# A fused Mamba-2 and PReLU kernel: wider filler matmuls, two clamps moved to VectorE, a transposition issued later, products of pair 1 in another bank

## The chip, the cores and the metric

The kernel runs on one core of one Trainium2 chip. A core has five engines that work side by side, each taking its own instructions in order: TensorE (PE in the profile; its weight loads are shown apart as PEld), VectorE (DVE), ScalarE (ACT), GpSimd (POOL) and SyncE (SP), which here only issues DMA transfers. Engines wait for each other through semaphores. The metric is the device time of one execution in microseconds (us). Less is better.

## The reference

Two blocks follow each other.

1. A state-space block. For 4 batches and 8 heads, 768 tokens are taken in chunks. Inputs are x (32 wide), B and C (16 wide) and a decay a per token, clipped to 1e-6..1. In a chunk, `y_intra = ((C B^T) * L) x`, where L[i, j] is the product of the decays from j+1 to i for j <= i and 0 above. To it comes `y_inter = (C state) * decay_to_i`. The state then becomes `decay_full * state + sum_j B_j x_j decay_from_j`.
2. The result, as 3072 tokens of 256 features, goes through `h = x w_in` (256 x 2048), `g = max(h, 0) + alpha * min(h, 0)` and `g w_out` (2048 x 256). The weights come in as 64-bit floats and are brought to 32 bits on the chip.

## The kernel before

The order of every engine is written out by hand: the order of the calls in the source is the order of each engine's instructions. Nothing is reordered by cost. Tiles come from pools with a fixed number of buffers, and an allocation waits for the readers of the buffer's earlier tile.

**Tiles and stages.** The 24 chunks of 128 tokens are taken in 12 pairs. Four chunks (512 tokens) make a group for the second block. The first two pairs are done by `first_two()` with half chunks of 64 tokens, beside the start of the second block. Then a loop over `f` = 4..15 (line 1431) does the hidden blocks of group 0 (`hidden`, `output`) with later pairs' stages (`ssm`) between them. Groups 1 to 5 follow in the loop at line 1482, with a scheme that needs seven products in place of eight (`quad`, `product`, `combine`). The change touches only what comes before and around the start of the first loop.

**A weight piece** is 128 x 2 x 256 numbers. There are 16: `w_in` 0, 1, then alternately `w_in` and `w_out`. Its raw words are loaded by SyncE (`load_weights`, L253). `convert_a` takes the magnitude on ScalarE (L269), clamps it on GpSimd (L271), and prepares the low half on ScalarE (L276 for `w_in`, L279 for `w_out`; the latter reads `g_mul` and `g_add`, which `slope_signs` writes on GpSimd, L391). `sign` takes the sign on VectorE (L290), `convert_b` shifts and joins on VectorE (L300), and `convert` adds the halves on GpSimd (L322). `convert_next` calls `convert` for the next piece in order and may issue another load.

**Fillers.** `keep_warm` (L330) issues matmuls of ones that nothing reads, at four places before and in `first_two`: eight, six and four of 128 columns and two of 128 columns.

**Pair 1 in `first_two`.** `spread` (L859) brings decays to four banks `sp`, `scan` (L865) runs over them on VectorE, `turned` transposes B and C (L835) and copies them (L841 to L849). `added` (L887) makes the products B^T x for the states, in banks `dps`. `states` (L902) chains them on VectorE, `gram_of` (L874) makes C B^T, `times` (L879) multiplies it by the scanned decays, `mask` (L908) spreads the states, and `x_products` (L921) and `state_products` (L933) give y, which `copy_out` (L941, L942) puts into `xT`.

**Hidden blocks.** `hidden_two(g, f, t0, hp, after)` does blocks f and f + 1 for 256 tokens (L1088), calling `after` behind each of its four products; `scaled` (ScalarE, L1098) and L1109 (VectorE) apply the PReLU and free the bank `hp`. There are two such banks, taken in turn: `hidden_two(0, 0, 2 * Q)`, `hidden_two(0, 2, 2 * Q)` (lines 1418 and 1420), then `hidden(0, 4)` (L1073, with L1076 and L1077), `hidden(0, 5)` and so on.

**Rows.** `rows_scan(0)` (L457) scans the decays of 96 rows backwards on VectorE; `rows_turn` (L497) transposes the result on TensorE and copies it on ScalarE (L504) to `prt`, which `pair_loads` (L528, GpSimd) multiplies with B to `bn`. `rows_products` (L434) scans forwards and stores the result `rpf` to DRAM (L437, `pf`), from where `load_products` (L167) reads it spread over the partitions as `ap`. The stage of pair 2 that makes its states (L637) multiplies by `ap`.

**Pair 2's products** (`products_bc`, L737) use four banks, the last of them one of the two `hp` banks, in turn after `hidden(0, 7)`.

Of the kernel before, what the change touches and what calls it, by code (L numbers as in the profile page):

```python
# [9 lines left out]
F32 = mybir.dt.float32  # L10
U32 = mybir.dt.uint32
U16 = mybir.dt.uint16
ALU = mybir.AluOpType
ACTF = mybir.ActivationFunctionType

F64_INF, F64_ZERO = (struct.unpack("f", struct.pack("I", w))[0] / 8
                     for w in (0x47F00000, 0x38000000))
# [5 lines left out]
def kernel(  # L23
# [25 lines left out]
    nc = tc.nc  # L49
# [4 lines left out]
    batch, H, S, D = x.shape  # L54
    N = B.shape[-1]
    P = 128
    Q = 128
# [9 lines left out]
    GT = GC * Q  # L67
    NG = NCH // GC
    NP = NCH // 2
    LATE = 4  # L70
    WARM = 8
    NQ = NF // 2
    NZ = NF // 4
    HM = d_model // 2
# [180 lines left out]

    parts = {}

    def convert_a(dst, src, sg):

        if src.dtype == F32:  # L260
            return
        raw = raws.pop(id(dst))
        hi = raw[:, :, :, 1]
        half = raw.rearrange("p k w t -> p k (w t)").bitcast(U16)
        half = half.rearrange("p k (w t) -> p k w t", t=4)[:, :, :, 1]
        t = wtp.tile([P, 2, WQ], U32, name="wt")
        g = wtp.tile([P, 2, WQ], F32, name="wg")

        nc.scalar.activation(out=t.bitcast(F32), in_=hi.bitcast(F32), func=ACTF.Abs, scale=0.125)  # L269

        nc.gpsimd.tensor_scalar(out=t.bitcast(F32), in0=t.bitcast(F32), scalar1=F64_INF,  # L271
                            scalar2=F64_ZERO, op0=ALU.min, op1=ALU.max)


        if sg is None:
            nc.scalar.activation(out=g, in_=half, func=ACTF.Copy, scale=2.0**-11, bias=2.0**25)  # L276
        for i in range(2 if sg is not None else 0):
            f = slice(sg + i, sg + i + 1)
            nc.scalar.activation(out=g[:, i], in_=half[:, i], func=ACTF.Identity,  # L279
                                 scale=g_mul[:, f], bias=g_add[:, f])  # L280
        parts[id(dst)] = hi, t, g

    signs = {}

    def sign(dst, src, sg):

        if src.dtype == F32 or id(dst) in signs:
            return
        r = wtp.tile([P, 2, WQ], U32, name="wr")
        nc.vector.tensor_single_scalar(out=r, in_=parts[id(dst)][0], scalar=SIGN,  # L290
                                       op=ALU.bitwise_and)
        signs[id(dst)] = r

    def convert_b(dst, src, sg):

        if src.dtype == F32:
            return
        sign(dst, src, sg)
        (hi, t, g), r = parts.pop(id(dst)), signs.pop(id(dst))
        nc.vector.scalar_tensor_tensor(out=r, in0=t, scalar=3, in1=r,  # L300
                                       op0=ALU.logical_shift_left, op1=ALU.bitwise_xor)
        parts[id(dst)] = r, g
# [24 lines left out]
    def keep_warm(to, n, cols=2 * Q):  # L327

        for i in range(n):
            nc.tensor.matmul(to[:, :cols], warm.to_broadcast([P, P]), warm.to_broadcast([P, cols]),  # L330
                             start=True, stop=True, skip_group_check=True)

    keep_warm(ps_h.tile([P, GT], F32, name="hp"), WARM, Q)
    ident = const.tile([P, P], F32, name="ident")
    make_identity(nc, ident)

# [115 lines left out]
    def rows_scan(i):  # L452

        d0 = held[i]
        nc.vector.memset(d0[:, Q : Q + 1], 0.0)
        pr = prep.tile([RW, Q], F32, name="pr")
        nc.vector.tensor_tensor_scan(out=pr[:, ::-1], data0=d0[:, 1 : Q + 1][:, ::-1],  # L457
                                     data1=ends[:RW, ::-1], initial=0.0,
                                     op0=ALU.mult, op1=ALU.add)
        return pr  # L460
# [55 lines left out]
    def pair_loads(gp):  # L516

        b, c = divmod(2 * gp, CPB)
        nat, abc, xt, ap = loads["p", gp]

        bn = work.tile([P, 2, H * N], F32, name="bn")
        i, bi = divmod(b, 2)
        if gp >= HALF:
            pj = prt[i].rearrange("p (j b m h) -> p j b m h", j=2, b=2, h=H)[:, :, bi, c // 2]
        else:
            pj = (prt[i if gp >= NB else "short"]
                  .rearrange("p (b h c) -> p b c h", b=2, h=H)[:, bi, c : c + 2])
        nc.gpsimd.tensor_tensor(  # L528
            out=bn.rearrange("p k (h n) -> p k h n", h=H),
            in0=nat[:, 0].rearrange("p k (h n) -> p k h n", h=H),  # L530
            in1=pj.unsqueeze(3).to_broadcast([P, 2, H, N]), op=ALU.mult)
        return bn
# [8 lines left out]
    def spare():  # L541

        return ps_h.tile([P, GT], F32, name="hp", tag="hp")
# [272 lines left out]
    def first_two():  # L816
# [47 lines left out]
        def scan(i, r, t):  # L864
            nc.vector.tensor_tensor_scan(out=dec[i][:, r], data0=t[:, : 2 * Q], data1=ident_q,  # L865
                                         initial=0.0, op0=ALU.mult, op1=ALU.add)
# [15 lines left out]
        def added(dps, bn, xt):  # L882
            for k in range(2):
                for r in range(4):
                    rs = slice(32 * r, 32 * r + 32)
                    for j, hs in enumerate(halves):
                        nc.tensor.matmul(dps[j][rs, k], bn[hs, k, rs],  # L887
                                         xt[hs, k, 2 * r * D : 2 * (r + 1) * D],
                                         start=True, stop=True, tile_position=(HQ * j, 32 * r),
                                         skip_group_check=True)  # L890
# [4 lines left out]
        def states(i, dps, pf, cs=range(4)):  # L895
            for c in cs:
                if i == 0 and c == 0:
                    nc.scalar.copy(out=new[0][:, 0], in_=dps[0][:, 0])
                    continue
                e = (c + 1) * HQ - 1  # L900
                old = new[i][:, c - 1] if c else new[0][:, 3]
                nc.vector.scalar_tensor_tensor(out=new[i][:, c], in0=old, scalar=pf[:, e : e + 1],  # L902
                                               in1=dps[c % 2][:, c // 2], op0=ALU.mult,
                                               op1=ALU.add)
# [85 lines left out]


        hp = spare()
        keep_warm(hp, 6, Q)
        gram_of(bc0, cz0, sp)
        dps = dps_in([hp, tp])
        added(dps, bn0, xt0)
# [4 lines left out]
        for r in (2, 3):  # L1001
            times(0, r, sp[r])
        z1 = first_a(loads["a", 1], nc.vector, lent[1][:, 2:])
        convert_a(*pieces[0])
        sign(*pieces[0])
        convert_b(*pieces[0])
        y = places([ss(), ss()], [hp, tp])
        x_products(y, xt0, 0, (0,))
        sp = [bank(r) for r in range(4)]
        keep_warm(sp[0], 4, Q)  # L1010
        x_products(y, xt0, 0, (1,))
        state_products(y, 0, cd0)
        spread(z1, sp)
        keep_warm(sp[3][:, 2 * Q :], 2, Q)
        convert_next()
        convert_a(*pieces[1])
        xts[0] = xtp.tile([P, KC, GT], F32, name="xT")
        copy_out(0, y)
        sign(*pieces[1])
        convert_b(*pieces[1])  # L1020
        prelu_of = {0: hidden_two(0, 0, 0, spare())}


        for r in range(4):
            scan(1, r, sp[r])
        bn1 = pair_loads(1)
        convert_next(first=False)
        mask(0, slice(3, 4))
        own = [ss(), ss()]
        bc1, cz1 = turned(nat1, own[0], nc.scalar)  # L1030
        dps = [t.rearrange("p (k m) -> p k m", k=2)
               for t in (own[1][:, 2 * Q : 2 * Q + 4 * D], sp[3][:, : 4 * D])]
        added(dps, bn1, xt1)
        cd1 = decayed_c(bc1, pf1)

        def among(i, k):
            if (i, k) == (0, 1):
                states(1, dps, pf1)
                gram_of(bc1, cz1, sp)
                one_at_a_time(1, range(3))  # L1040
                for r in range(4):
                    times(1, r, sp[r])
                prelu_of[0]()
                convert_a(*pieces[2])
                sign(*pieces[2])
            if (i, k) == (1, 0):
                y = places(own, [bank(0), bank(1)])
                x_products(y, xt1, 1)
                state_products(y, 1, cd1)
                copy_out(1, y)  # L1050

        prelu_of[2] = hidden_two(0, 2, 0, spare(), among)
        convert_next(first=False)
        mask(1, slice(3, 4))
        slope_signs()
        prelu_of[2]()
        pr = rows_scan(0)
        rows_products()
        load_products(NB, loads["p", NB][3])
        rows_turn(0, pr)  # L1060
        state[0] = new[1][:, 3]
        masked[0] = sm[1][:, 3]
        early[0] = 16
# [337 lines left out]
    def convert_next(first=True, **kw):  # L1401


        i = done[0]
        if i < len(pieces):
            convert(*pieces[i], **kw)
            if first and i and i + 2 < len(pieces):
                convert_a(*pieces[i + 2])
            if loaded[0] == i + 6:
                load_next()  # L1410
        done[0] += 1
# [6 lines left out]
    hidden_two(0, 0, 2 * Q, spare())()  # L1418
    convert_next(first=False)
    rest = hidden_two(0, 2, 2 * Q, spare())  # L1420
    convert_a(*pieces[4])
    rest()
    identity_bank()
# [133 lines left out]
```

## Time and profile before

| what | us |
|---|---|
| median of 3 executions | 364.32 |
| lowest and highest of them | 363.22, 364.84 |
| the profiled execution's own time | 365.23 |
| its span, first to last instruction | 362.4 |
| TensorE busy | 353.2 (97%) |
| VectorE busy | 238.7 (66%) |
| GpSimd busy | 203.5 (56%) |
| ScalarE busy | 171.3 (47%) |

The profile lists for each instruction its engine, its source line (L12 is line 12), the operation, what it writes and reads, its start and its length. "Idle before" is time in which the engine had nothing to run, with the engine that ended it. The chain of work that ended last is followed back from the last instruction, at each step to what released it by the recorded semaphore events; such a releaser is inferred and can be a bystander that ended at the same time. The granted clock is the share of TensorE's full clock. "SPq" is SyncE issuing a transfer; "issue" is time for which the profile shows no cause.

### The profile page before, as it was taken

What the parts mean: (1) busy time and instruction counts of PE and PEld (TensorE: products, weight loads), DVE (VectorE), ACT (ScalarE), POOL (GpSimd) and SP (SyncE); (2) the same over time, 40 slices, a digit from 0 to 9 for tenths busy, and PEclk for the clock granted to TensorE, in tenths of its full rate; (3) what the DMA queues carried; (4) which work ended last, traced back from release to release, by engine and by line L of the source; (5) the groups of instructions that cost most, each with busy time, mean ns of one, the idle gap of its engine ahead of it and who ended that gap; (6) DMA issues with size and microseconds to landing.
All of it is one profiled execution on the core that took longest, in us unless ns stands there. A gap on an engine that the chain in (4) does not pass through costs nothing.

```text
span 362.4 us, 7825 instructions
## 1 busy us (share of the span) xinstructions
PE 353.2 (97%) x3011; PEld 290.5 (80%) x3011; DVE 238.7 (66%) x487; ACT 171.3 (47%) x386; POOL 203.5 (56%) x226
## 2 busy tenths in 40 slices
PE   8869999999999999999999999999999999999996
PEld 7647656667888888888888888888888888888885
DVE  7874795989846756766656866657866634743363
ACT  2345756634345435535535535535535534453431
POOL 5853658669965947544546545537545546334510
PEclk9996999999999999999999999999999999999999
DMA  7889689704535510510540530530201001001102
GB/s 118 178 172 328 221 162 344 164 5 76 171 64 135 98 39 25 107 46 11 109 88 12 108 87 14 112 81 17 58 2 31 0 2 29 2 0 32 31 0 58
DMA packets 105581, 30.24 MB, mean 83 GB/s; under 512 B 79896, under 2 KB 101448, under 8 KB 105544
## 3 DMA queue, kind: packets, MB, share of 16 engines
q1 hardware_dynamic: 105160, 29.57, 35.5%
q8 instruction: 23, 0.38, 0.4%
q10 hardware_dynamic: 384, 0.18, 0.2%
q14 instruction: 14, 0.11, 0.1%
HBM read 26.32 MB, written 3.42 MB: 82 GB/s over the span
## 4 chain that ended last, share of the span: by engine, by line
PE 87%; DVE 4%; DMA 4%; SPq 2%; POOL 1%; ACT 1%; issue 1%; DVEq 0%; POOLq 0%
PE bank L1194 33%; PE hp L1219 28%; PE bank L1120 6%; PE ss L1219 6%; PE hp L1073 3%; DMA pf<-rpf 2%; PE hp L1088 2%; PE ss L782 1%; DVE dec L562 1%; DMA raw<-in_moe_w_in_dram 1%; PE ss L726 1%; PE bank L1187 1%; PE ss L774 1%; DVE wr L300 1%; PE ss L800 1%; DMA ap<-pf 1%
## 5 line engine op out<-in xcount | busy, mean ns | idle before, releaser
L1276 POOL TENSOR_TENSOR gt<-gt 128x512 f32<-128x512 f32 x58 | 74.1, 1278 | 21.1 <-DVE gt L1204 16.3
L1194 PE MATMUL bank<-gt,w_out 128*128 128x256 f32 x320 | 83.5, 381 | 0.0
L1194 PEld LDWEIGHTS bank<-gt,w_out 128*128 128x128 f32 x320 | 60.1, 190 | 9.2 <-issue 1.0
L1204 DVE SCALAR_TENSOR_TENSOR gt<-hp,s_mul,gt 128x256 f32<-128x256 f32 x96 | 42.0, 478 | 29.1 <-ACT gt L1202 26.8
L1266 POOL TENSOR_TENSOR gt<-gt 128x512 f32<-128x512 f32 x20 | 25.4, 1270 | 62.9 <-DVE gt L1204 49.3
L1202 ACT ACTIVATE gt<-hp,s_alpha 128x256 f32<-128x256 f32 x96 | 40.3, 471 | 34.6 <-PE hp L1219 31.5
L1194 PE MATMUL bank<-gt,ws 128*128 128x256 f32 x224 | 55.9, 379 | 0.0
L1194 PEld LDWEIGHTS bank<-gt,ws 128*128 128x128 f32 x224 | 42.3, 190 | 5.6
L1219 PE MATMUL hp<-xs,w_in 128*128 128x256 f32 x160 | 41.9, 384 | 0.0
L1219 PE MATMUL hp<-xs,ws 128*128 128x256 f32 x160 | 41.1, 379 | 0.0
L1245 DVE TENSOR_TENSOR hp<-hp,u 128x512 f32<-128x512 f32 x20 | 14.0, 699 | 35.2 <-ACT u L1243 35.2
L1219 PEld LDWEIGHTS hp<-xs,ws 128*128 128x128 f32 x160 | 30.3, 190 | 4.3 <-POOL xs L1161 0.2
L1219 PEld LDWEIGHTS hp<-xs,w_in 128*128 128x128 f32 x160 | 29.7, 190 | 4.5
L1120 PE MATMUL bank<-w_out,gt 128*128 128x256 f32 x128 | 31.1, 385 | 0.4 <-POOL w_out L322 0.4
L1120 PEld LDWEIGHTS bank<-w_out,gt 128*128 128x128 f32 x128 | 23.6, 190 | 7.2 <-issue 3.1
L1219 PE MATMUL ss<-xT,w_in 128*128 128x256 f32 x96 | 24.6, 379 | 0.0
L640 POOL TENSOR_TENSOR sm<-state,bmask 128x256 f32<-128x256 f32 (+1 forms) x10 | 6.2, 618 | 29.8 <-DVE state L637 29.8
L1073 PE MATMUL hp<-xT,w_in 128*128 128x512 f32 x48 | 22.7, 596 | 0.0
L556 DVE TENSOR_TENSOR_SCAN dec<-abc,bank 128x192 f32<-128x192 f32 x48 | 22.7, 522 | 0.0
L1234 ACT COPY m<-hp 128x512 f32<-128x512 f32 x8 | 4.7, 586 | 35.7 <-PE hp L1219 35.7
L1243 ACT COPY u<-hp 128x512 f32<-128x512 f32 x20 | 11.7, 585 | 19.4 <-PE hp L1219 19.4
L1204 DVE SCALAR_TENSOR_TENSOR gt<-c,s_mul,gt 128x256 f32<-128x256 f32 x40 | 20.6, 555 | 0.0
(233 smaller groups left out, 620.3 us busy)
## 6 DMA issues: line engine op xcount, KB each, us to landing
abc<-z SPq DMA_DIRECT2D x24, 192.0 KB
raw<-in_moe_w_in_dram SPq DMA_DIRECT2D x8, 512.0 KB
raw<-in_moe_w_out_dram SPq DMA_DIRECT2D x8, 512.0 KB
abc<-z SPq DMA_DIRECT2D x8, 512.0 KB
out_dram<-o_sb SPq DMA_DIRECT2D x32, 64.0 KB
nat<-in_B_dram SPq DMA_DIRECT2D x26, 64.0 KB
nat<-in_C_dram SPq DMA_DIRECT2D x24, 64.0 KB
xt<-in_x_dram SPq DMA_DIRECT2D x12, 128.0 KB
```

Of the source, the lines that this page charges most:

```text
L556: nc.vector.tensor_tensor_scan(out=dv[:, o : o + SQ], data0=abc[k][:, s : s + SQ], data1=ident_p[0][:, :SQ], initial=0.0, op0=ALU.mult, op ...
L1073: nc.tensor.matmul(hp, w_in[:, k, f * P : (f + 1) * P], xts[g][:, k], start=(k == 0), stop=(k == KC - 1))
L1088: nc.tensor.matmul(hp[:, i * nt : (i + 1) * nt], w_in[:, k, fs], xts[g][:, k, ts], start=(i == 0 and k == 0), stop=(k == KC - 1), skip_gro ...
L1120: nc.tensor.matmul(pos[0][t // 2][:, t % 2], gt[:, t * Q : (t + 1) * Q], w_out[:, f], start=(f == 0 and t % 2 == 0), stop=(f == NF - 1), s ...
L1194: nc.tensor.matmul(ms[g][i][:, h], w, blocks[g, z][n][:, p], start=(q == 0 and h == 0), stop=(q == NQ - 1), skip_group_check=True)
L1202: nc.scalar.mul(o[:, p], h[:, p], s_alpha[:, fs[p]])
L1204: nc.vector.scalar_tensor_tensor(out=o[:, p], in0=h[:, p], scalar=s_mul[:, fs[p]], in1=o[:, p], op0=ALU.mult, op1=ALU.max)
L1219: nc.tensor.matmul(to[:, p], w(2 * z + p), b, start=start and p == 0, stop=True, skip_group_check=True)
L1243: nc.scalar.copy(out=u2, in_=A)
L1245: nc.vector.tensor_tensor(out=Y, in0=Y, in1=u2, op=ALU.add)
L1266: nc.gpsimd.tensor_tensor(out=tc_, in0=g22, in1=g12, op=ALU.subtract)
L1276: eng.tensor_tensor(out=o, in0=x0, in1=x1, op=ALU.subtract)
```

## The change

- The fillers become two, one and one of 512 columns and one of 256 (in `keep_warm`'s default width).
- `convert_a` gets an argument `by`. For pieces 0 and 1 the clamp is done by VectorE, with the sign ahead of it. GpSimd clamps the other pieces as before.
- In `first_two`, the addition of piece 1 (`convert_next`) stands ahead of `pair_loads(1)` instead of behind it.
- The second half of pair 1's `dps` lies in bank `sp[0]` instead of `sp[3]`, and `added` and `states` of pair 1 are called behind the first product of `hidden_two(0, 2, 0)`; before, `added` stood ahead of it and `states` behind the second.
- `convert_b` of piece 2 is called by name ahead of `convert_next`, which called it itself.
- `rows_turn(0)` is called behind `hidden_two(0, 0, 2 * Q)` and the matmuls of `hidden_two(0, 2, 2 * Q)`; before, it was the last call of `first_two` that used an engine.

```diff
--- before.py
+++ after.py
@@ -68,7 +68,7 @@
     NG = NCH // GC
     NP = NCH // 2
     LATE = 4
-    WARM = 8
+    WARM = 2
     NQ = NF // 2
     NZ = NF // 4
     HM = d_model // 2
@@ -255,7 +255,7 @@
 
     parts = {}
 
-    def convert_a(dst, src, sg):
+    def convert_a(dst, src, sg, by=nc.gpsimd):
 
         if src.dtype == F32:
             return
@@ -268,8 +268,11 @@
 
         nc.scalar.activation(out=t.bitcast(F32), in_=hi.bitcast(F32), func=ACTF.Abs, scale=0.125)
 
-        nc.gpsimd.tensor_scalar(out=t.bitcast(F32), in0=t.bitcast(F32), scalar1=F64_INF,
-                            scalar2=F64_ZERO, op0=ALU.min, op1=ALU.max)
+        parts[id(dst)] = hi, t, g
+        if by is nc.vector:
+            sign(dst, src, sg)
+        by.tensor_scalar(out=t.bitcast(F32), in0=t.bitcast(F32), scalar1=F64_INF,
+                         scalar2=F64_ZERO, op0=ALU.min, op1=ALU.max)
 
 
         if sg is None:
@@ -278,7 +281,6 @@
             f = slice(sg + i, sg + i + 1)
             nc.scalar.activation(out=g[:, i], in_=half[:, i], func=ACTF.Identity,
                                  scale=g_mul[:, f], bias=g_add[:, f])
-        parts[id(dst)] = hi, t, g
 
     signs = {}
 
@@ -330,7 +332,7 @@
             nc.tensor.matmul(to[:, :cols], warm.to_broadcast([P, P]), warm.to_broadcast([P, cols]),
                              start=True, stop=True, skip_group_check=True)
 
-    keep_warm(ps_h.tile([P, GT], F32, name="hp"), WARM, Q)
+    keep_warm(ps_h.tile([P, GT], F32, name="hp"), WARM, GT)
     ident = const.tile([P, P], F32, name="ident")
     make_identity(nc, ident)
 
@@ -990,7 +992,7 @@
 
 
         hp = spare()
-        keep_warm(hp, 6, Q)
+        keep_warm(hp, 1, GT)
         gram_of(bc0, cz0, sp)
         dps = dps_in([hp, tp])
         added(dps, bn0, xt0)
@@ -1001,41 +1003,40 @@
         for r in (2, 3):
             times(0, r, sp[r])
         z1 = first_a(loads["a", 1], nc.vector, lent[1][:, 2:])
-        convert_a(*pieces[0])
-        sign(*pieces[0])
+        convert_a(*pieces[0], by=nc.vector)
         convert_b(*pieces[0])
         y = places([ss(), ss()], [hp, tp])
         x_products(y, xt0, 0, (0,))
         sp = [bank(r) for r in range(4)]
-        keep_warm(sp[0], 4, Q)
+        keep_warm(sp[0], 1, GT)
         x_products(y, xt0, 0, (1,))
         state_products(y, 0, cd0)
         spread(z1, sp)
-        keep_warm(sp[3][:, 2 * Q :], 2, Q)
+        keep_warm(sp[3][:, 2 * Q :], 1)
         convert_next()
-        convert_a(*pieces[1])
         xts[0] = xtp.tile([P, KC, GT], F32, name="xT")
         copy_out(0, y)
-        sign(*pieces[1])
+        convert_a(*pieces[1], by=nc.vector)
         convert_b(*pieces[1])
         prelu_of = {0: hidden_two(0, 0, 0, spare())}
 
 
         for r in range(4):
             scan(1, r, sp[r])
+        convert_next(first=False)
         bn1 = pair_loads(1)
-        convert_next(first=False)
         mask(0, slice(3, 4))
         own = [ss(), ss()]
         bc1, cz1 = turned(nat1, own[0], nc.scalar)
         dps = [t.rearrange("p (k m) -> p k m", k=2)
-               for t in (own[1][:, 2 * Q : 2 * Q + 4 * D], sp[3][:, : 4 * D])]
-        added(dps, bn1, xt1)
+               for t in (own[1][:, 2 * Q : 2 * Q + 4 * D], sp[0][:, : 4 * D])]
         cd1 = decayed_c(bc1, pf1)
 
         def among(i, k):
+            if (i, k) == (0, 0):
+                added(dps, bn1, xt1)
+                states(1, dps, pf1)
             if (i, k) == (0, 1):
-                states(1, dps, pf1)
                 gram_of(bc1, cz1, sp)
                 one_at_a_time(1, range(3))
                 for r in range(4):
@@ -1050,14 +1051,14 @@
                 copy_out(1, y)
 
         prelu_of[2] = hidden_two(0, 2, 0, spare(), among)
+        convert_b(*pieces[2])
         convert_next(first=False)
         mask(1, slice(3, 4))
         slope_signs()
         prelu_of[2]()
-        pr = rows_scan(0)
+        held["pr"] = rows_scan(0)
         rows_products()
         load_products(NB, loads["p", NB][3])
-        rows_turn(0, pr)
         state[0] = new[1][:, 3]
         masked[0] = sm[1][:, 3]
         early[0] = 16
@@ -1418,6 +1419,7 @@
     hidden_two(0, 0, 2 * Q, spare())()
     convert_next(first=False)
     rest = hidden_two(0, 2, 2 * Q, spare())
+    rows_turn(0, held["pr"])
     convert_a(*pieces[4])
     rest()
     identity_bank()
```

## The prediction

> **What bounds the kernel now.** I read the page's busy shares first (TensorE 97% of the span), then the chain that ended last in the first 60 us, then the timelines of SyncE and TensorE there, then busy time by stretch. After 52.30 us TensorE is busy 306.66 of 310.10 us and nothing of the change is left, so everything is decided before that. The chain (start us, length us, what):
>
> ```profile
> 26.52 0.43 DVE pr L457
> 26.95 0.14 issue
> 27.08 0.39 PE ss L497
> 27.48 3.48 PE hp L1088 x8
> ...
> 32.73 0.55 DVE wr L300
> 33.28 6.17 DMA pf<-rpf
> ...
> 39.46 2.86 DMA ap<-pf
> ...
> 42.41 0.28 DVE state L637
> 42.70 2.33 DVE dec L562 x4
> ...
> 50.98 1.28 POOL w_out L322
> ...
> 52.31 1.99 PE bank L1120 x8
> ```
>
> TensorE stands for the turning of the rows (L497), which waits for their scan; then the path leaves TensorE for a store, a load, VectorE and GpSimd, and returns at 52.31. By stretch (length; busy and count of TensorE, its weight loads, VectorE, ScalarE, GpSimd; granted clock; DMA share; GB/s):
>
> ```profile
> 24.00:27.10 3.10, 0.71 (x5) 0.34 (x4) 2.55 (x8) 1.14 (x4) 1.77 (x2) 0.87 0.82 100
> 27.10:33.20 6.10, 6.10 (x15) 4.93 (x16) 2.12 (x5) 2.66 (x6) 1.42 (x4) 0.51 0.98 299
> 33.20:46.80 13.60, 13.60 (x58) 8.38 (x58) 10.00 (x18) 9.86 (x20) 8.06 (x10) 1.00 0.79 269
> 46.80:52.30 5.50, 5.07 (x28) 2.90 (x28) 5.40 (x11) 2.21 (x4) 3.26 (x4) 1.00 0.72 101
> ```
>
> TensorE idles 2.39 us and then runs 6.1 us at half clock: a loss of about 2.4 + 3.0 = 5.4 us. That looks like the prize. But VectorE is busy 5.40 of the 5.50 us before 52.30, so there it is the bound. What starts its run? SyncE's timeline and one line each of VectorE's and TensorE's:
>
> ```profile
> 28.12 3.86 SPq L253 DMA_DIRECT2D raw<-in_moe_w_in_dram  x1
> 32.09 0.59 SPq L253 DMA_DIRECT2D raw<-in_moe_w_out_dram  x1
> 32.77 0.41 SPq L253 DMA_DIRECT2D raw<-in_moe_w_in_dram  x1
> 33.28 0.41 SPq L437 DMA_DIRECT2D pf<-rpf  x1
> 39.46 0.60 SPq L167 DMA_DIRECT2D ap<-pf  x1
> ```
> ```profile
> 42.41 0.28 DVE L637 SCALAR_TENSOR_TENSOR state<-gt,ap,ss 128x64 f32<-128x64 f32 x1 [1.49 <-DMA ap<-pf]
> ```
> ```profile
> 46.86 0.48 PE L737 MATMUL hp<-cz,bc 32*128 32x256 f32 x1
> ```
>
> rpf was written at 27.54, yet its store is issued at 33.28, behind three weight loads in SyncE's queue, the first of which takes 3.86 us to issue with the DMA engines 98% busy. So I don't believe the chain's link from L300 to the store: L300 doesn't write rpf, and it ended at the same moment. The store is late because of DMA, not TensorE. It lands at 39.46, its copy ap at 42.3, and VectorE, which takes its work in order, waits for it 1.49 us with everything behind it: scans, conversions, and the activation of hidden block 6 (46.14 to 46.80), which frees the bank that L737 takes at 46.86.
>
> **What the Trainium skill says.** "TensorE: Matmul & The Clock Gate", Part 1 (the HAM clock gate): the clock falls to half after an idle window of about 3.4 us and returns after a busy one; the windows run freely. The trace agrees: by single microseconds the mean clock is 0.66 in 26 to 27, 0.50 to 33, 0.93 in 33 to 34, so half speed from about 26.3 to 33.1, two windows of 3.4, after a window with 1.6 us of waiting in it. "SBUF — State Buffer", Who interferes with whom: VectorE's tensor_scalar in a two-port mode and a GpSimd instruction exclude each other. The trace agrees: the sign of piece 1 (L290) takes 1.39 us beside GpSimd's addition (13.55 to 14.82) and 0.41 alone.
>
> **The change part by part.** Times below "after" are estimates from the rows of before.
>
> *Fillers.* Columns: 8x128 and 2x512 are the same 1024; 6x128 becomes 512; 4x128 and 512 are equal; 2x128 and 256 too. Cold, 16 passes took 3.75 us (234 ns each); two passes of 512 columns each cost four times the columns with fewer gaps, some 3.5, so the first spread starts up to 0.2 us earlier (4.3 for 4.51). The second group ends about 0.64 us earlier (1.50 falls to 0.86), but the products behind it wait until 8.54 for cz (VectorE): nothing. The third is followed by products that wait for VectorE until 11.5: nothing. Cover gone, these would bring at most 1 us. The other side: less filling, and a clock that falls before 16 us; the idle there would be under 1 us, and idles of 0.9 us at 13.2 and 17.8 left the clock at 1.00. I take none.
>
> *Clamps of pieces 0 and 1.* GpSimd loses two L271 (0.77 and 0.68); VectorE gains two of 0.4 (nearest row: L290, 0.41, same shape), at worst 1.4 beside a GpSimd addition. The hop over GpSimd goes: piece 0 is added at about 13.2 for 13.55, piece 1 at 16.05 for 16.77, because the addition now also stands ahead of bn (1.14). Bn then ends near 18.0 for 16.8, and no load moves: the only DMA among the moved calls is convert_next's weight load, which keeps its place on SyncE.
>
> *Added products in another bank, and behind a first matmul.* They waited until 18.70 for the scan of the fourth bank (0.89 us idle). Bank 0 is scanned 1.8 us earlier, so bn releases them, at about 18.05. With the earlier w_in, states, gram and products of pair 1 come some 1.0 to 1.1 us earlier: xT is done near 23.5 for 24.58. Landing of w_in piece 2 (ScalarE waits for it until 21.26) doesn't move, and its conversion comes 0.9 us earlier. The explicit second half of its conversion stands where it stood: nothing.
>
> *Rows turned later.* One transposition (0.39) and one ScalarE copy (0.24) go behind eight matmuls; no DMA goes with them, and the next reader, bn of pair 2, needs it only at 36. TensorE runs L1088 from 23.5 at full clock: 4 x 0.43 = 1.71 us, the next four from 25.2 (their bank is freed by L1109 at about 25.1), the transposition at 26.9. Then hidden block 4 needs the bank of the first four. Its release is queued on ScalarE behind the conversion of piece 3, whose L279 waits for g_mul and g_add, which stand on GpSimd behind piece 2 and a mask: GpSimd ends about 26.75, L279 27.9, L1098 28.75, L1109 29.7. So TensorE idles from 27.3 to 29.7: the stall of 2.4 us goes to another place, and block 4 starts at 29.7 for 33.66.
>
> *What it is worth at 52.31.* From block 4 to L737 before: 46.7 - 33.7 = 13.0 us, so TensorE arrives at 42.7 at full clock. There it waits for VectorE's 46.80, which hangs on ap at 42.3. From L637 VectorE has 50.91 - 42.41 = 8.5 us without a gap, GpSimd 1.3, and w_out comes at 52.3 as before. All 4 us are lost again. The sum: 0.2 + 1.1 + 2.4 + 3.0 off, less 2.4 new stall, less 4.2 waiting at L737, that is 0.
>
> And a price: 2.4 + 4.2 us of idling are two new reasons for half clock. If a window after 46.86 is slow, 3.41 us do 1.7 us of work; slack is 0.44 (the wait ahead of 52.31), so the end comes 1.27 later. Two windows: 2.96. If the first stall already halves the clock, 1.7 to 3.0 of the wait at L737 is used up and the second fall may not come. The kernel before can meet such windows too, in executions with another phase.
>
> **Rivals.**
> *Absorbed (forecast).* For it: VectorE's 1.49 us wait for a transfer and 98% DMA share. Change between 0 and +1.8; I take 0.7, about half of the 1.27, since the phase decides for both kernels.
> *The gain reaches the end.* If the chain is right and the store is released by VectorE's work, L300 of piece 3 comes 3 us earlier (30.3 for 33.28) and so does the end: 361.3. With the whole 5.4: 358.9. Against it: rpf was ready 5.7 us before, and SyncE's issue of 3.86 us has twins at 9.44 (3.54) and 19.39 (3.59), on first-used buffers that nothing has to free.
> *Half clock behind L737 for two windows* (slower): the place is gram, output 3 and hidden block 8, 5.0 us of work. It decides from 2.3 us lost: 2.3 - 0.44 = 1.86. At 3.4 lost: 364.3 + 2.96 = 367.3.
> *The change doesn't do what it says:* the wait for the rows goes to the bank of hidden block 4. That I hold likely; it alone gives 0.
>
> **How the numbers follow.** The profiled execution took 365.23 (span 362.40 and 2.83 around it); the median is 364.32, 0.91 lower. The changes above are differences, and I put them on the median: 364.32 + 0.7 = 365.0. Absorbed 0.57 (own range 363.6 to 366.1), two slow windows or a like loss 0.27, gain arrives 0.16. The range leaves out the far half of the gain (below 362.4) and the far end of the half-clock case (above 367.1). A measurement of this kernel tells about 0.5%, 1.8 us, from no change: faster is below 362.5, slower above 366.1.
>
> **What would show it.** Right: no idle ahead of L497; 2 to 3 us idle ahead of L1073's first group near 30, ended by L1109; several us idle ahead of L737's hp, ended by L1077; pf still issued near 33.3, L637 still near 42.4 with a wait on ap of 3 us or more; L1120 at 52.3 or later. Half clock in 47 to 50 shows the price. Wrong: pf issued or landing more than 1 us earlier, L637 with it, or L737 reached after 46.8 without idling.

## The result, and the profile after

The kernel after takes 364.27 us (median of 22 executions, 362.70 to 365.95), the kernel before 364.61 beside it (22 executions). The ratio is 0.9985, 95% interval 0.997 to 1.0. The medians differ by about 0.3 us, no change that this measurement can tell from none. The profiled execution after took 363.67 us, with a span of 362.0; before it was 365.23 and 362.4.

The chain that ended last, after (start us, length us, what; lines have moved by one or two: L1074, L1078, L1121, L302, L324 and L639 are L1073, L1077, L1120, L300, L322 and L637 of before):

```profile
27.99 1.12 ACT wg L282 x2
29.11 0.52 ACT gt L1099 x2
...
32.10 0.50 SPq L253
32.71 0.41 SPq L253
33.21 6.02 DMA pf<-rpf
39.24 2.62 DMA ap<-pf
41.96 0.28 DVE state L639
42.24 2.33 DVE dec L564 x4
...
50.53 1.28 POOL w_out L324
51.86 1.99 PE bank L1121 x8
```

The turning of the rows is off the path, as it should be, but the store of the rows' products is still issued at 33.2, lands at 39.2, and the rest follows as before. The chain now names SyncE's queue ahead of the store, and no longer VectorE's L300: that instruction (L302 now) ended at 31.33, 1.9 us ahead of the store. So in the profile of before it was a bystander: it had ended at the moment at which the store was issued.

The same stretches of time as before (length; busy and count of TensorE, its weight loads, VectorE, ScalarE, GpSimd; granted clock; DMA share; GB/s):

```profile
24.00:27.10 3.10, 3.06 (x15) 2.24 (x14) 2.58 (x8) 1.66 (x5) 1.82 (x2) 1.00 0.66 96
27.10:33.20 6.10, 3.78 (x11) 2.07 (x10) 3.92 (x8) 4.11 (x10) 3.03 (x6) 0.82 0.98 305
33.20:46.80 13.60, 13.58 (x64) 8.15 (x63) 7.95 (x14) 8.67 (x16) 7.29 (x9) 0.95 0.80 268
46.80:52.30 5.50, 5.05 (x24) 2.83 (x17) 5.29 (x11) 1.66 (x4) 2.81 (x4) 1.00 0.83 118
```

The idle 2.4 us have moved from 24 to 27.1 (busy 3.06 of 3.10 now) into 27.1 to 33.2 (busy 3.78 of 6.10). In the last stretch, 46.8 to 52.3, VectorE is busy 5.29 of 5.50 us again. TensorE's timeline, ahead of pair 1's products, ahead of hidden block 4, in pair 2's products and at output 4, with what ended the idle time:

```profile
20.39 0.70 PE L876 MATMUL bank<-cz,bc 32*64 32x128 f32 x32 [0.90 <-DVE gt L904]
```
```profile
30.88 3.63 PE L1074 MATMUL hp<-xT,w_in 128*128 128x512 f32 x4 [2.32 <-DVE gt L1110]
```
```profile
45.68 0.48 PE L739 MATMUL ss<-cz,bc 32*128 32x256 f32 x1
...
46.41 0.48 PE L739 MATMUL hp<-cz,bc 32*128 32x256 f32 x1
...
51.86 1.99 PE L1121 MATMUL bank<-w_out,gt 128*128 128x256 f32 x8 [0.44 <-POOL w_out L324]
```

And VectorE's wait for the transfer, 1.49 us before:

```profile
41.96 0.28 DVE L639 SCALAR_TENSOR_TENSOR state<-gt,ap,ss 128x64 f32<-128x64 f32 x1 [2.04 <-DMA ap<-pf]
```

Output 4 is the fifth group of products with `w_out` (`output(0, 4)`), the one at 52.31 before. The piece of `w_out` that it waits for is finished on GpSimd, behind VectorE's run.

Block 4 waits 2.32 us for its bank and then takes 3.63 us where 1.88 is its usual length: half clock. So TensorE comes to pair 2's products only 1.0 us earlier (45.68 for 46.68), waits for VectorE's activation of block 6, and output 4 starts at 51.86 for 52.31. From the state to output 4 it is 51.86 - 41.96 = 9.90 us; before, 52.31 - 42.41 = 9.90. The 0.45 us come from ap, which landed that much earlier in this execution; the two spans differ by 0.4 us too.

### The profile page after: what moved, and what is told of

The parts are those of the page before. It is cut to its first block, busy times and chain, and to the rows that moved or that the text cites. A ratio compares the mean times of both kernels' runs of the same rounds, so it can differ in the third digit from the quotient of the medians.

```text
span 362.0 us, 7766 instructions
## 1 busy us (share of the span) xinstructions
PE 351.4 (97%) x2981; PEld 284.0 (78%) x2981; DVE 238.9 (66%) x489; ACT 171.0 (47%) x386; POOL 202.2 (56%) x224
## 4 chain that ended last, share of the span: by engine, by line
PE 86%; DVE 4%; DMA 4%; SPq 2%; POOL 1%; ACT 1%; issue 1%; DVEq 0%; POOLq 0%
PE bank L1195 33%; PE hp L1220 28%; PE bank L1121 6%; PE ss L1220 6%; PE hp L1074 3%; DMA pf<-rpf 2%; PE ss L784 1%; DMA raw<-in_moe_w_in_dram 1%; DVE dec L564 1%; PE ss L728 1%; PE bank L1188 1%; DVE wr L302 1%; PE ss L776 1%; PE ss L802 1%; DMA ap<-pf 1%; POOL w_in L324 1%
## 5 line engine op out<-in xcount | busy, mean ns | idle before, releaser
L1220 PEld LDWEIGHTS hp<-xs,w_in 128*128 128x128 f32 x160 | 29.7, 190 | 4.5
L1121 PE MATMUL bank<-w_out,gt 128*128 128x256 f32 x128 | 31.1, 385 | 0.4 <-POOL w_out L324 0.4
L1121 PEld LDWEIGHTS bank<-w_out,gt 128*128 128x128 f32 x128 | 23.6, 190 | 7.2 <-issue 3.1
L1074 PE MATMUL hp<-xT,w_in 128*128 128x512 f32 x48 | 24.5, 635 | 2.3 <-DVE gt L1110 2.3
```

The lines of the kernel that those rows point to most:

```text
L1074: nc.tensor.matmul(hp, w_in[:, k, f * P : (f + 1) * P], xts[g][:, k], start=(k == 0), stop=(k == KC - 1))
L1121: nc.tensor.matmul(pos[0][t // 2][:, t % 2], gt[:, t * Q : (t + 1) * Q], w_out[:, f], start=(f == 0 and t % 2 == 0), stop=(f == NF - 1), s ...
L1220: nc.tensor.matmul(to[:, p], w(2 * z + p), b, start=start and p == 0, stop=True, skip_group_check=True)
```

## The experiments

The theory: VectorE's run from the state of pair 2 to output 4 starts when ap lands, ap hangs on SyncE's queue and the DMA engines, and TensorE's gain ahead of it is lost in waiting. This wait for ap is called the gate below. The rivals: TensorE's own time decides; half clock after longer idling costs more than the change brings; another transfer is next.

In every run these starts are read (us): the first of pair 2's products, the first that needs the last of the four banks (which VectorE's activation of block 6 frees), the state of pair 2, and output 4.

| run | first product | last bank | state of pair 2 | output 4 | state to output 4 |
|---|---|---|---|---|---|
| before | 46.68 | 46.86 | 42.41 | 52.31 | 9.90 |
| after | 45.68 | 46.41 | 41.96 | 51.86 | 9.90 |
| reorder | 42.72 | 46.56 | 42.12 | 54.24 | 12.12 |
| reorder_filled | 46.42 (fillers from 42.88) | 47.72 | 43.28 | 53.17 | 9.89 |
| store_late | 45.53 | 48.23 | 43.79 | 53.69 | 9.90 |
| turn_alone | 47.20 | 48.78 | 44.34 | 54.23 | 9.89 |
| store_early | 44.46 | 44.48 | 38.62 | 49.08 | 10.46 |
| store_early_before | 45.09 | 45.12 | 39.26 | 49.72 | 10.46 |
| both | 42.58 | 42.60 | 36.92 | 47.20 | 10.28 |
| both_bank2 | 42.06 | 42.08 | 36.31 | 46.69 | 10.38 |
| turn_and_store | 46.35 | 46.38 | 40.52 | 50.98 | 10.46 |
| turn_store_reorder | 42.39 | 42.41 | 37.60 | 47.49 | 9.89 |

Each row is one execution. Where output 4 waits for VectorE's run, the last distance is 9.9 whatever TensorE does before it. In reorder it is longer, because TensorE ran at half clock there. In the last six rows, which all have the earlier store, the bank is free when TensorE comes.

**reorder: give TensorE the 2.3 us.** Block 4 waits for a bank whose release is queued on ScalarE behind the conversion of piece 3 (L282, which waits for g_add on GpSimd). The conversion is called later:

```diff
-    convert_a(*pieces[3])
-    sign(*pieces[3])
     hidden_two(0, 0, 2 * Q, spare())()
+    convert_a(*pieces[3])
+    sign(*pieces[3])
     convert_next(first=False)
```

> The kernel after, with the conversion of piece 3 called behind the first matmuls and activation of hidden_two(0, 0, 2Q) instead of ahead of them. This takes away the new 2.3 us stall ahead of hidden block 4. Theory (the gain is absorbed: VectorE waits for the decay products ap, which come by DMA): no change to the kernel before within 0.4%; block 4 starts near 28.5 without a stall, TensorE reaches the products of pair 2 at 41 to 43 and idles there 3 to 5 us until VectorE has done hidden block 6, whose turn still comes behind the state of pair 2 at about 42; output 4 not before 51.8. Rival 1 (TensorE's own time decides): 2.3 us of stall and 1.4 us of half clock go, the end comes 3 to 4 us earlier than in the kernel after, about 360.5. Rival 2 (half clock after the longer idling): output 4 comes 1.3 to 3 us later, 365.5 to 367.5.

365.54 us; ratio to before 1.0005 (0.9984 to 1.0025). TensorE's and VectorE's timelines and the last stretch:

```profile
46.56 0.79 PE L739 MATMUL hp<-cz,bc 32*128 32x256 f32 x1 [3.13 <-DVE gt L1078]
```
```profile
42.12 0.28 DVE L639 SCALAR_TENSOR_TENSOR state<-gt,ap,ss 128x64 f32<-128x64 f32 x1 [5.06 <-DMA ap<-pf]
```
```profile
46.80:52.30 5.50, 5.50 (x19) 3.96 (x20) 5.34 (x10) 0.00 (x0) 2.95 (x4) 0.50 0.64 77
```

The stall ahead of block 4 is gone and TensorE is 3 us further ahead, and all of it is lost: VectorE waits 5.06 us for ap, TensorE 3.13 us for VectorE. Rival 1 falls. Then comes what rival 2 said: the whole stretch runs at half clock, and output 4 starts 2.2 us later against the state than in every run that is gated by VectorE at full clock (12.12 for 9.90). In the time this shows in the direction only; the intervals of this run and the kernel after overlap. With the loss by half clock in it, the time of this run can't show the absorption; the two waits in its trace do.

**reorder_filled: the same, with work that nobody needs in the gap.**

```diff
             gram = {r: ss_tile() if r < small else spare() for r in range(4)}
+            if gp == 2:
+                keep_warm(gram[0], 4, GT)
```

> The kernel with the conversion of piece 3 called later, and four fillers of 512 columns ahead of the products of pair 2, where TensorE idled 3.7 us and then ran at half clock for 5.5. They write a bank that the products overwrite. Theory of the half clock: useless work keeps the clock up, output 4 comes near 52.0 instead of 54.2, 363.0 instead of 365.5. Rival (the 2.3 us are lost to VectorE or to a transfer): no change, 365.5, or a little later.

364.24 us, ratio 0.9994 (0.9975 to 1.0013). TensorE's timeline and the stretch:

```profile
42.88 3.61 PE L332 MATMUL ss<-const-float32-1.0 128*128 128x512 f32 x8
```
```profile
46.80:52.30 5.50, 4.90 (x28) 2.80 (x22) 5.40 (x11) 0.00 (x0) 2.94 (x4) 1.00 0.87 159
```

The clock stays at 1.00 and the distance is 9.89 again, so in this pair of executions the 2.2 us go with the half clock. In this execution ap was late by 1.2 us (state at 43.28, its store issued 1.0 us later than in reorder), so output 4 came at 53.17, not at 52.0, and the time missed the expected 363.0. In the time the two runs are not told apart. The fillers use up the 3 us that TensorE was ahead, so this run tests the half clock and not rival 1.

**store_early and store_early_before: take the wait for ap away.** The clamp of the rows goes to an earlier place on GpSimd and the forward scan to an idle half microsecond of VectorE near 5 us; the store then goes behind that of z, and the load of ap behind the spread decays, ahead of three weight loads in SyncE's queue. (In `rows_products` the store is dropped and `rpf` returned.)

```diff
         z0 = first_a(ap0, nc.vector, lent[1][:, :2])
+        rows_clamp(0)
...
         clamp(nc.vector, starts_a[:, ::HQ], ap0[:, ::HQ])
+        rpf0 = rows_products()
...
-        rows_clamp(0)
         rows_out(0)
+        nc.sync.dma_start(out=scratch["pf", 0], in_=rpf0)
...
         load_spread(2, *divmod(4, CPB))
+        load_products(NB, loads["p", NB][3])
...
-        rows_products()
-        load_products(NB, loads["p", NB][3])
```

> The kernel after, with the rows' forward products computed at about 5 us instead of 27 and stored right behind the store of z, and ap loaded right behind the spread decays of pair 2, ahead of three weight loads. Theory: VectorE no longer waits for ap (2.0 us in the kernel after), the state of pair 2 comes at about 40.0 for 42.0, TensorE goes into the products of pair 2 at 45.7 without waiting, needs 5.0 us from there and reaches output 4 at 50.7 for 51.9: 1.1 us earlier, 363.2. Rival 1 (ap doesn't matter, TensorE's own time decides): same as the kernel after, 364.3. Rival 3 (the store can't come earlier than the queue lets it, the wait only moves to the next transfer): state earlier but output 4 at 51.9, 364.3.

> The kernel before with the same earlier store and load of the rows' products. Theory: TensorE comes to the products of pair 2 at 46.7, as it did, so only the 0.44 us wait ahead of output 4 and some 0.1 ahead of the last of the products go: 0.4 to 0.6 us, 364.1 or no measurable change. If the wait for ap alone decided (no part for TensorE), the gain would be 1.5 us or more, 363.1.

On the kernel after: 361.02 us, ratio to before 0.9892 (0.9859 to 0.9924). On the kernel before: 363.32 us, 0.9956 (0.9936 to 0.9976). SyncE's, TensorE's and VectorE's timelines of the first:

```profile
16.67 1.48 SPq L987 DMA_DIRECT2D pf<-rpf  x1
...
28.82 3.20 SPq L167 DMA_DIRECT2D ap<-pf  x1
```
```profile
31.36 1.96 PE L1074 MATMUL hp<-xT,w_in 128*128 128x512 f32 x4 [2.22 <-DVE gt L1110]
```
```profile
49.08 1.90 PE L1121 MATMUL bank<-w_out,gt 128*128 128x256 f32 x8
```
```profile
38.62 0.27 DVE L638 SCALAR_TENSOR_TENSOR state<-gt,ap,ss 128x64 f32<-128x64 f32 x1
```

VectorE doesn't wait for ap any more, and TensorE waits nowhere between block 4 and output 4. Both gains are larger than expected (3.3 us below the kernel after for 1.1; 1.6 below the one before for 0.5). In these executions the reason is the clock: block 4 ran at full clock after its stall (1.96 us for 3.63), and in the kernel before half clock ended earlier (mean 0.72 in 27.1 to 33.2 for 0.51). Whether the medians have the same reason is open. The 1.6 us on the kernel before are also what the rival named (ap alone decides, 1.5 us or more). Its trace speaks against that rival: TensorE comes to the products at 45.09, 1.6 us earlier than before, and waits nowhere from there to output 4.

What the pair shows: with the gate away, the change is worth 363.3 - 361.0 = 2.3 us by the medians (the intervals don't overlap); with it, nothing. The two profiled executions show only 0.64 us of it (output 4 at 49.08 and 49.72), since that of store_early_before was the fastest of its 15, 361.58.

**store_late: make the gate 1.3 us later.** One more load of 512 KB, whose data are overwritten later, ahead of the store:

```diff
         scratch["pf", 0] = dr.tile([RW, Q], F32, name="pf0")
+        nc.sync.dma_start(out=w_out[:, NF - 4 :].rearrange("p f m -> p (f m)").bitcast(U32),
+                          in_=moe_w_out.bitcast(U32).rearrange("(p f) m -> p (f m)", p=P)[:, : 4 * WQ])
         nc.sync.dma_start(out=scratch["pf", 0], in_=rpf)
```

> The kernel after with one more load of 512 KB in SyncE's queue just ahead of the store of the rows' products; its data are overwritten later and never used. Theory: the store, ap, the state of pair 2 and everything behind it on VectorE come about 1.3 us later (512 KB at the 390 GB/s that this stretch moves), output 4 at 53.2 for 51.9, 365.6. Rival 1 (TensorE's own time decides): no change, 364.3.

365.93 us, ratio 1.0032 (1.0008 to 1.0056), on a chip where before took 364.96; the interval lies above that of the kernel after (0.997 to 1.0). VectorE's and TensorE's timelines:

```profile
43.79 0.28 DVE L641 SCALAR_TENSOR_TENSOR state<-gt,ap,ss 128x64 f32<-128x64 f32 x1 [4.01 <-DMA ap<-pf]
```
```profile
48.23 0.48 PE L741 MATMUL hp<-cz,bc 32*128 32x256 f32 x1 [1.99 <-DVE gt L1080]
```

State and output 4 come 1.83 us later than in the kernel after (1.3 expected), with the same 9.90 between them, although TensorE comes to the products no later (45.53 for 45.68). One trace alone would not show this: in the other runs with the late store the state came anywhere from 41.96 to 44.34. The time shows it. Here a transfer ahead of the store costs time at the end, and TensorE's idle time doesn't.

**turn_alone: the later turning alone, on the kernel before.**

```diff
-        pr = rows_scan(0)
+        held["pr"] = rows_scan(0)
...
-        rows_turn(0, pr)
...
     rest = hidden_two(0, 2, 2 * Q, spare())
+    rows_turn(0, held["pr"])
```

> The kernel before with one part of the change alone: the rows are turned behind the matmuls of hidden_two(0, 2, 2Q). Theory: the 2.39 us of idling ahead of the turning go, some 2.3 us ahead of hidden block 4 take their place, output 4 stays between 51.8 and 52.5: same as the kernel before within 0.3%, 364.7. Rival 1: 2.4 us or more faster, 362.2 or less. If this alone does what the whole change does in the trace from 24 us on, the other parts carry nothing.

364.72 us, ratio 0.9999 (0.9978 to 1.002). TensorE:

```profile
34.10 1.96 PE L1072 MATMUL hp<-xT,w_in 128*128 128x512 f32 x4 [2.33 <-DVE gt L1108]
```

The stall of 2.33 us is there without any other part of the change. All absolute times of this execution are some 2 us late, since TensorE was at half clock for a while before 24 us (mean 0.52 in 16 to 20, 0.50 in 20 to 22); output 4 missed its expected window for this reason, and the distance is 9.89.

**both, both_bank2: the gate and the stall together.** `both` is the kernel after with the edits of reorder and store_early; `both_bank2` adds

```diff
-               for t in (own[1][:, 2 * Q : 2 * Q + 4 * D], sp[0][:, : 4 * D])]
+               for t in (own[1][:, 2 * Q : 2 * Q + 4 * D], sp[2][:, : 4 * D])]
```

> The kernel after with both edits: the earlier store and load of the rows' products, and the conversion of piece 3 behind hidden_two(0, 0, 2Q). Theory: the stall ahead of hidden block 4 (2.2 us) was worth nothing while VectorE waited for ap, and is worth its length now: TensorE comes to the products of pair 2 near 42.4 without waiting there, VectorE's activation of block 6 ends before that, output 4 near 47.5: 1.5 to 2.2 us off the 361.0 of the earlier store alone, 359.2. Rival 1 (another transfer gates next, a weight piece or the spread decays): 361, with VectorE or ScalarE waiting for DMA ahead of block 6.

> As the run with both edits, and the second half of pair 1's added products in bank 2 instead of bank 0. The step of the prediction that failed: the products C B^T of pair 1 write bank 0 first, so they wait until the states of pair 1 have been read from it (0.90 us of idling in the kernel after), and xT is done no earlier than before. Theory: with bank 2 the first four of them go ahead, the rest wait as before; xT comes 0.2 to 0.4 us earlier and, with TensorE deciding, so does the end: 358.9. Rival (the wait is for something else): nothing moves.

358.82 us, ratio 0.9832 (0.9806 to 0.9857), and 358.79 us, 0.9833 (0.9806 to 0.9859): both are faster than the two kernels of this document. The edit of reorder, worth nothing alone, brings 2.2 us here. The stretch of `both`, and TensorE's timeline of `both_bank2` in pair 1's products:

```profile
33.20:46.80 13.60, 13.60 (x66) 8.31 (x64) 12.88 (x21) 8.60 (x16) 8.74 (x11) 1.00 1.00 309
```
```profile
19.60 0.45 PE L875 MATMUL bank<-cz,bc 32*64 32x128 f32 x8
20.48 0.67 PE L875 MATMUL bank<-cz,bc 32*64 32x128 f32 x24 [0.43 <-DVE gt L903]
```

TensorE is busy without a gap and at full clock, while VectorE is busy 12.88 of 13.60 us. With bank 2 a quarter of the products goes ahead, the wait falls from 0.90 to 0.43, and xT is done at 24.48 for 24.99. Of these 0.51 us, 0.28 were there already when the states ended (20.42 for 20.70); the bank brought the other 0.23, within the 0.2 to 0.4 expected. In the time it isn't seen.

**turn_and_store, turn_store_reorder: is it the turning alone?** The edits of turn_alone and store_early on the kernel before, and with them that of reorder.

> The kernel before with the rows turned later (one part of the change) and the earlier store and load of the rows' products. The whole change with the earlier store was 361.0, the kernel before with it 363.3: the change is worth 2.3 us there. Theory: the later turning alone carries this, because the other parts brought xT no further (24.5 for 24.6): 361.0, ratio 0.989. Rival (fillers, clamps or the other bank carry part of it): between 361.5 and 363.3.

> As the run before, and the conversion of piece 3 behind hidden_two(0, 0, 2Q). With the whole change this was 358.8. Theory: the same here, 358.8 (ratio 0.983), with TensorE never idle between 25 and 50; fillers, clamps and bank give nothing even where TensorE decides, since xT is as early without them. Rival: 359.3 or more.

362.43 us, ratio 0.9913 (0.9887 to 0.994), and 359.42 us, 0.9844 (0.9818 to 0.9871). With the whole change they were 0.9892 and 0.9832. Both medians missed the theory's figures (361.0 and 358.8) and lie where the rivals had put them (361.5 to 363.3; 359.3 or more). But the intervals overlap with those of the whole change both times. With the earlier store, the turning alone brings 0.43% (0.9956 to 0.9913) of the whole change's 0.64%, about two thirds, and its interval overlaps with that of store_early_before too. So whether fillers, clamps and bank carry the remaining 0.1 to 0.2% is not settled.

In the profile of the first, block 4 took 3.61 us, half clock, where that of store_early took 1.96. In that of the second TensorE should never have been idle between 25 and 50, by the theory; it waited 0.37 us at 31.41 for `w_out`, and at output 4 for VectorE's run again:

```profile
47.49 1.99 PE L1119 MATMUL bank<-w_out,gt 128*128 128x256 f32 x8 [0.32 <-POOL w_out L322]
```

The state came at 37.60 there and at 36.92 in `both`, without a wait for ap in either; what delayed VectorE's work ahead of it was not tested.

## Why the prediction was right, point by point

The forecast was 365.0 with no change as the likeliest; the time is 364.27, inside the absorbed case's own range of 363.6 to 366.1. The mechanism is shown by store_late (the gate later: slower), store_early (the gate away: the change is worth 2.3 us) and reorder (TensorE 3 us ahead: its trace shows it waiting, and the time doesn't fall). The 0.7 us that the forecast added for half clock did not come; the median is 0.3 lower instead, within noise. Two terms on TensorE's side were wrong as well (below). They did no harm to the forecast, because what TensorE gains or loses there is absorbed.

- *The chain's link from L300 to the store is false.* Right: L302 ended 1.9 us ahead of the store after, and the store kept its 33.2.
- *The stall goes to hidden block 4.* Right: 2.4 us predicted, 2.32 measured, and by the queue that was named (ScalarE's L282 at 27.99, behind g_add). It starts 1.3 us later than the 27.3 predicted (28.56), because of the next point: the conversion of piece 2, and with it g_add, stands behind xT.
- *xT 1.0 to 1.1 us earlier.* Wrong: 24.53 for 24.58. Conversions (w_in piece 1 at 16.15, predicted 16.05) and added products (18.25, predicted 18.05) came as worked out. The step that failed is "states, gram and products come some 1.0 to 1.1 us earlier": pair 1's C B^T starts with bank 0 and now waits until the states have been read from there (0.90 us, L904). With the products in the fourth bank, 12 of the 32 recorded matmuls of C B^T went ahead of that wait. VectorE's multiplication by them starts at 21.07 for 21.12. both_bank2 halves the wait. In no run was xT done before 24.29.
- *Clamps on VectorE.* Right: 0.43 and 0.41 us for the 0.4 taken; the sign of piece 1 still takes 1.38 us beside GpSimd's addition (13.39 to 14.66) for 0.41 alone. The Trainium skill has it so in "SBUF — State Buffer", Who interferes with whom: a tensor_scalar of VectorE in a two-port mode and an instruction of GpSimd lock each other out. That this instruction ran in such a mode, no run here shows.
- *Fillers.* The first group took 3.38 us after, but 3.75 in store_early and both, as before: the 0.2 us were not a gain of wider fillers. The wait "issue" of 0.89 us in the middle of the second spread is missing after (its 32 products run from 12.46 without a gap), and then TensorE waits 0.93 us for w_in instead. Which part of the change took the "issue" away was not tested.
- *4.2 us of waiting at pair 2's products.* Mis-sized: 0.55 (the last bank is taken 0.73 behind the first product, 0.18 before). TensorE arrived at 45.7, not at 42.7: block 4 began at 30.88 for 29.7, and half clock took 1.75 in it (3.63 for 1.88). The sum had named this branch, in which the first stall uses up the second, but its figure was that for full clock. With the measured terms TensorE gains 1.00 us up to the first product and loses 0.55 there, which leaves the 0.45 of output 4.
- *The price of half clock.* 1.27 or 2.96 us in the prediction, 2.2 in reorder. In the kernel after the second fall didn't come (the clock is 1.00 from 46.8 to 52.3), so the 0.7 added for it was not there.
- *The clock and the page.* The prediction says that the trace agrees with the idle window of about 3.4 us. The lengths do: half speed lasted 6.8 us before, two windows, and about 3.4 in the kernel after (mean 0.51 in 31 to 32, 0.50 to 34, 0.79 in 34 to 35). The trigger doesn't: by the prediction's own figures the window ahead of the fall was idle for 1.6 us only.
- *The signs.* As named came: no idle ahead of L497, 2 to 3 us ahead of block 4, pf issued at 33.21, and no sign of being wrong. Smaller than named were the idle ahead of the last bank (0.55 for several us) and the wait on ap (2.04 for 3 or more), and output 4 came at 51.86, not at 52.3 or later.

## What to carry to other kernels

Before a stall on the busiest engine is mended, ask what that engine meets next: here a transfer decided, which TensorE's 97% doesn't show, and the mended stall turned into two new waits. A store through DRAM in a full queue took the time of what stood ahead of it here (6.0 us for 48 KB, 7.1 with another 512 KB ahead), so issue such a store, and the load behind it, as soon as their data can exist. After one gate is gone, an edit that was worth nothing can be worth its length, as reorder's was (2.2 us): try it again.

## What the runs showed of the hardware that was not expected

- The same stall of 2.2 to 2.3 us ahead of block 4 led to half clock in some executions and not in others: 3.63 (after), 3.53 (store_late) and 3.61 us (turn_and_store) for its four products, but 1.96 in store_early and turn_alone. The Trainium skill, "TensorE: Matmul & The Clock Gate", Part 1, puts the idle window at about 3.4 us and says that the windows run freely; here an idle time of 2.2 to 2.3 us sufficed in three executions of five. That it depends on where the windows fell fits these figures, but no run shows where they begin. In these five executions one such stall added either nothing or 1.6 to 1.7 us (3.53 to 3.63 for 1.96).
- Kernels without the gate and the stall seem to repeat better: `both` lies between 358.60 and 358.96 in 5 executions, both_bank2 between 358.32 and 359.40 in 6, turn_store_reorder between 358.82 and 360.75 in 4, the kernel before between 363.22 and 366.58 in 22. The counts are unequal, and that the gate's landing and the clock make the spread is argued, not shown.
